# One weight load split over two DMA queues, and most filler matmuls left out, in a fused attention and soft-MoE kernel

## The chip, the cores and the metric

The kernel runs on one core of a Trainium2 chip. The core has five engines with instruction streams of their own: TensorE (PE in the profile, with its weight loads listed as PEld), VectorE (DVE), ScalarE (ACT), GpSimd (POOL) and SyncE (SP). They wait for each other through semaphores. Data comes from and goes to HBM through 16 DMA engines; a DMA is issued by SP, ACT or POOL, and the profile lists what each of these issued as a queue of its own: q1 for SP, q10 for ACT and q0 for POOL.

The metric is the device time of one execution, in microseconds; lower is better.

## The reference

The first stage is attention over 8 batches and 8 heads, 576 positions of 64 elements. Heads 0 to 3 look back over a window of 32 positions, heads 4 to 7 over every fourth of the last 128. The second stage is a soft mixture of experts on the 4608 tokens of 512 elements that come out: softmax weights over all tokens for 32 slots, two matmuls for each of 8 experts on its 4 slots, and softmax weights over the slots that spread the result back over the tokens.

```python
scores = scale * np.matmul(q, k.transpose(0, 1, 3, 2))
scores = np.where(masks[None, :, :, :], scores, -1000000000.0)
...
attn = attn / (np.sum(attn, axis=-1, keepdims=True) + 1e-09)
return np.matmul(attn, v).astype(np.float32)
...
logits = x @ phi
...
slot_input = d.T @ x
...
for e in range(E):
    h = np.maximum(slot_input[e] @ w1[e], 0.0)
    slot_out[e] = h @ w2[e]
...
return (c @ slot_out).astype(np.float32)
```

All inputs and the output are fp32 in HBM; on the chip the matmuls run in bf16.

## The kernel before

**Units.** Attention runs in 8 units: two batches times one kind of head (plain or dilated). `load_unit` (L433) brings q, k and v of a unit into one of three staging buffers `stg`, with three or six DMAs from POOL's queue that turn fp32 into bf16 on the way. The first unit is loaded in two halves of three DMAs each by `load_first` (L457). For each unit `st_T` (L627) transposes the staged data on TensorE (L643, L637) and ScalarE copies them to `TT` (L671); `st_S` makes scores (L689) and exponentials (L696); `st_V`, `st_P` and `st_X` make the output of attention; `st_L` makes the logits of a batch and adds to the slot inputs. A staging buffer can be loaded for unit u+3 when the transposes of unit u have read it, so the loads at L449 and L442 wait on POOL for TensorE.

**Weights.** All 16 expert weights stay in SBUF as bf16, each in a `home`: w1 of experts 0 to 6 in `WD`, the others in staging buffers and in `TT` once attention no longer needs them. `wload` (L479) and `wpair` (L860) load them from POOL's queue (L496, L874), in program order between the unit loads. The last of them, w2 of experts 6 and 7, come in pieces: first the columns 0 to 255, then the columns 256 to 511.

**The head.** One piece of a weight does not come through POOL. Half of w1 of expert 0 is loaded as fp32 by SP (L517, 1024 KB) into `pre`, which is the space of the later w1 of expert 6, and ScalarE turns it into bf16 in two activations (L533). `moe_phi` follows on SP's queue (L520, 64 KB).

**The tail.** When the slot inputs are complete (`psA`, then `siT`), the first expert matmul (L954) makes `h`, which is transposed to `hT` (L972). The second expert matmul is cut into groups by `ffn2` (L1015, matmuls at L1028), each of which waits for the weight pieces that it reads. `half(0)` (L1068) then scales the slot outputs of columns 0 to 255 (L1062), multiplies them with `expT` (L1080, L1093), scales by rows (L1063 on ScalarE, L1062 and L1105 on VectorE) and stores 1536 tokens' half rows from SP's and ScalarE's queues (L1057). `half(1)` does the same for columns 256 to 511 when the last weight piece has landed, and L1137 with its scalings makes the other 3072 tokens, stored in four large DMAs.

**The order.** Operations are not run in the order of the program text. `Prog.schedule` (L159) is a planner that runs when the kernel is built: it keeps a clock of its own for each engine, takes durations from the `cost` of each operation and lets DMAs run one after the other at 421.5 KB per microsecond, and places the operation that can start first; among those within `TOL` of each other the smaller `key` goes first. POOL and SP keep the order of the program. `emit` (L277) writes out the instruction streams with the semaphore waits.

**The fillers.** `FILL` (L28) is a list of stretches of the planner's clock. Whenever TensorE would be idle there for more than 0.4 us before its next operation, the planner puts matmuls of a constant tile `wrm` into the gap (L244 to L260). Their result is never read. Each entry gives start, end, the modes of the following operation for which it holds, the time to be left free in the gap, and the assumed duration of one matmul. On the chip nothing holds a filler back until its planned time: it follows the TensorE operation ahead of it.

```python
ts = max(free[e], lo)
if not (ts < hi and lo < t0 and o.mode in modes and t0 - ts > 0.4):
    continue
...
n = min(int((t0 - ts - slack) / each + 0.05), 64)
```

Of the kernel before, what the change touches and what calls it, by code (L numbers as in the profile page):

```python
# [24 lines left out]
NU = 8  # L25
QB = 96
HALO = 32
FILL = ((1.5, 9.0, "hf", 0.4, 0.43), (9.5, 13.5, "hf", 0.6, 0.25), (13.5, 116.0, "h", 0.3, 0.216),  # L28
        (13.5, 24.0, "rf", 0.3, 0.216), (116.0, 147.0, "hrfc", 0.15, 0.216))


class DmaSem:
# [85 lines left out]
class Prog:  # L118
# [6 lines left out]
    def op(self, e, fn, r=(), w=(), a=(), alloc=(), cost=0.5, key=0.0, mode="f",  # L125
           sem=None, nbytes=0, after=(), ndma=1, n=0, port=False):
        o = Op(e, fn, cost, key, mode)
        deps = list(after)
        for b in r:
            deps += b.ready  # L130
        for b in w:
            b.fresh()
            deps += b.prev
        for b in a:
            deps += b.prev
        seen = set()
        for d in deps:
            if d.id not in seen:
                seen.add(d.id)
                o.deps.append(d)  # L140
        for b in r:
            b.reads.append(o)
        for b in list(w) + list(a):
            b.ready.append(o)
        o.wr = [b for b in list(w) + list(a) if b.pool is not None]
        for b in list(r) + list(w) + list(a):
            if b.pool is not None and b not in o.touch:
                b.left += 1
                o.touch.append(b)
        o.alloc = list(alloc)  # L150
        o.sems = sem
        o.bytes = nbytes
        o.ndma = ndma
        o.n = 2 * n
        o.port = port
        self.ops.append(o)
        return o
# [171 lines left out]
def bass_dilated_sliding_attn__then__soft_moe_slots_kernel(  # L329
# [12 lines left out]
    op = P.op  # L342
# [159 lines left out]
    b_pre = Buf()  # L502
# [7 lines left out]
    for i in range(3):  # L510
# [3 lines left out]
    op("dve", lambda g: g.memset(wrm[:], 1.0), w=[b_wrm], cost=0.2, key=-1)  # L514
    load_first(0)
    pre = WD[:, 6, :].bitcast(F32)
    op("sp", lambda e: [e.dma_start(  # L517
        pre, moe_w1[0].rearrange("(p c) f -> p (c f)", c=4)[:, 0:2048])],
       w=[b_pre], cost=0.1, sem=DmaSem(nc, "s_pre"), nbytes=1048576)
    op("sp", lambda e: [e.dma_start(phi_st[:], moe_phi.rearrange("(c p) s -> p c s", p=128))],  # L520
       w=[b_phist], cost=0.1, sem=s_phi, nbytes=65536)
    op("dve", lambda g: g.memset(id0[:], 0.0), w=[b_id0], cost=0.3)
# [474 lines left out]
    for x in range(2):  # L997
        def rsum(t, x=x):
# [5 lines left out]
           cost=0.8, key=K1 + x, after=[ffn1] if x else [])  # L1004
    op("dve", lambda vv: vv.reciprocal(rtok[:], bank(rs)[:, 0:N_TOK // 128]), r=[rs], w=[b_rtok],
       cost=0.2, key=K1 + 1)
# [117 lines left out]
    for i, (n, hs) in enumerate(((4, (3,)), (4, (4,)), (8, (5, 6)), (8, (7, 8)))):  # L1124
# [7 lines left out]
        for j0 in range(0, n, 2):  # L1132
            po = tile(psum, 2)

            def pe(t, d0=d0, n=n, j0=j0, po=po):
# [3 lines left out]
            key = K1 + 60 + 10 * i + j0  # L1139
            op("pe", pe, r=b_so + b_expT, w=[po], alloc=[po], cost=0.45,  # L1140
               key=key)
# [24 lines left out]

    P.schedule(filler, FILL)

# [39 lines left out]
```

## Time and profile before

| | us |
|---|---|
| median of 3 runs | 176.25 |
| lowest, highest | 175.98, 176.44 |
| the profiled execution | 176.83 |
| its span, first to last instruction | 175.1 |

| engine | busy us | share of the span | instructions |
|---|---|---|---|
| PE | 142.7 | 81% | 2305 |
| PEld | 102.4 | 58% | 2305 |
| DVE | 108.8 | 62% | 259 |
| ACT | 96.5 | 55% | 147 |
| POOL | 65.2 | 37% | 111 |

The span is what the profile shows; the profiled execution took 1.73 us more than it. The DMAs moved 41.29 MB, counted where they were written: 30.41 MB in POOL's queue, 8.98 MB in SP's and 1.57 MB in ScalarE's. HBM was read for 61.93 MB and written for 9.44 MB, since what POOL's queue loads is fp32 in HBM and bf16 on the chip.

The fillers (L1155) are 79 matmuls of 128x512 elements with 22.9 us of TensorE's busy time, 436 ns each in the mean. Twenty of them start before 7.5 us, 13 between 12.4 and 18.3 us, three at 23.8 to 24.4 us, two at 118.0 and 119.5 us, and 41 from 123.2 to 146.4 us.

How to read it: busy shares are means over stages with different limits. The parts that matter here are the DMA engines' busy share along the span and the chain of waits that ended last.

### The profile page before, as it was taken

To read this page: it belongs to the slowest core of one execution; us is meant where nothing else is said; L and a number is where in the kernel's file an instruction comes from. 1 tells how busy PE (TensorE), PEld (TensorE's weight loads), DVE (VectorE), ACT (ScalarE), POOL (GpSimd) and SP (SyncE) were. 2 spreads that over 40 slices of the span, in tenths; PEclk is the share of its full clock that TensorE was granted. 3 is DMA by queue.
4 is the path that set the end of the run, shared out by engine and by line. 5 is a ranking of instruction groups with operands and counts; after the bars stand their busy time and mean duration, and the time that the engine had idled before them with its cause. 6 is when DMAs were issued, how large, how long until landed. Compare 5 with 4: busy or idle time off the path is not lost.

```text
span 175.1 us, 5257 instructions
## 1 busy us (share of the span) xinstructions
PE 142.7 (81%) x2305; PEld 102.4 (58%) x2305; DVE 108.8 (62%) x259; ACT 96.5 (55%) x147; POOL 65.2 (37%) x111
## 2 busy tenths in 40 slices
PE   7759886889896999996998899988999898599000
PEld 2245465677795887794986698765575344343000
DVE  6620494599789799969469979997403002379400
ACT  2332836697885778887378596853111002589300
POOL 7980649506963053951020839689000000000000
PEclk9997999999999999999699999999999999879955
DMA  5999998999999999999999999999999999999997
GB/s 176 249 215 213 221 231 187 221 212 213 233 212 203 219 208 219 233 206 207 218 212 212 217 215 217 213 215 217 215 204 210 201 195 196 295 331 404 449 419 299
DMA packets 12694, 41.29 MB, mean 236 GB/s; under 512 B 2208, under 2 KB 8864, under 8 KB 9120
## 3 DMA queue, kind: packets, MB, share of 16 engines
q0 software_dynamic: 8128, 30.41, 86.4%
q1 hardware_dynamic: 2912, 8.98, 13.3%
q10 hardware_dynamic: 1632, 1.57, 2.7%
q8 instruction: 18, 0.29, 0.6%
q14 instruction: 4, 0.03, 0.0%
HBM read 61.93 MB, written 9.44 MB: 408 GB/s over the span
## 4 chain that ended last, share of the span: by engine, by line
DMA 46%; PE 19%; DVE 10%; POOL 9%; ACT 7%; issue 1%; POOLq 0%; DVEq 0%
DMA stg<-in_v_dram 29%; DMA TT<-in_moe_w_dram 17%; ACT PT L696 5%; PE ps L643 4%; PE ps L637 4%; DVE WD L1062 3%; POOL TT L496 2%; PE ps L798 2%; PE ps L714 2%; PE ps L689 2%; POOL stg L449 2%; DVE XB L754 2%; PE ps L743 1%; PE ps L1093 1%; POOL mask_p L540 1%; POOL stg L442 1%
## 5 line engine op out<-in xcount | busy, mean ns | idle before, releaser
L696 ACT ACTIVATE PT<-ps 128x768 bf16<-128x768 f32 x48 | 36.8, 818 | 11.2 <-PE ps L689 10.9
L671 ACT ACTIVATE TT<-ps 128x864 f32<-128x864 f32 x32 | 28.1, 902 | 19.0 <-PE ps L643 11.7
L754 DVE TENSOR_TENSOR XB<-ps,RV 96x768 bf16<-96x768 f32 x32 | 30.2, 945 | 0.4
L1155 PE MATMUL ps<-wrm 128*128 128x512 bf16 x79 | 22.9, 436 | 1.1 <-DVE wrm L514 1.1
L719 DVE COPY VN<-ps 128x768 bf16<-128x768 bf16 x32 | 16.9, 538 | 10.4 <-PE ps L714 10.0
L643 PE MATMUL ps<-ident,stg 96*128 96x96 bf16 x288 | 15.4, 216 | 5.7 <-DMA stg<-in_v_dram 5.3
L1063 ACT ACTIVATE WD<-ps,rtok 128x256 f32<-128x256 f32 (+1 forms) x22 | 10.7, 555 | 16.1 <-PE ps L1080 14.8
L689 PE MATMUL ps<-TT 64*128 64x96 bf16 x384 | 15.9, 204 | 3.8 <-ACT PT L696 2.0
L643 PEld LDWEIGHTS ps<-ident,stg 96*128 96x128 bf16 x288 | 14.2, 104 | 7.3 <-DMA stg<-in_v_dram 6.3
L610 POOL COPY stg<-stg 96x576 f32<-96x576 f32 x24 | 16.8, 699 | 1.5
L743 PE MATMUL ps<-VN,PT 128*128 128x65 bf16 x384 | 16.7, 194 | 0.5 <-ACT PT L696 0.3
L714 PE MATMUL ps<-ident,TT 128*128 128x128 bf16 x192 | 16.3, 223 | 0.7 <-ACT TT L671 0.2
L743 PEld LDWEIGHTS ps<-VN,PT 128*128 128x128 bf16 x384 | 14.1, 98 | 2.2 <-DVE XB L754 0.8
L689 PEld LDWEIGHTS ps<-TT 64*128 64x128 bf16 x384 | 9.7, 94 | 9.7 <-ACT PT L696 3.9
L1155 PEld LDWEIGHTS ps<-wrm 128*128 128x128 bf16 x79 | 8.1, 111 | 11.7 <-issue 5.7
L704 DVE TENSOR_TENSOR PT<-PT,mask_d 128x768 bf16<-128x768 bf16 x24 | 12.9, 569 | 0.0
L714 PEld LDWEIGHTS ps<-ident,TT 128*128 128x128 bf16 x192 | 11.3, 100 | 2.7 <-DVE VN L719 0.5
L704 DVE TENSOR_TENSOR PT<-PT,mask_p 128x768 bf16<-128x768 bf16 x24 | 12.6, 541 | 0.2
L771 PE MATMUL ps<-ident,XB 96*128 96x96 bf16 x192 | 11.4, 206 | 1.4 <-DVE XB L754 1.2
L449 POOL DMA_DIRECT2D stg<-in_q_dram x8 | 4.1, 526 | 22.4 <-PE ps L643 22.4
L637 PE MATMUL ps<-ident,stg 96*128 96x96 bf16 x216 | 10.9, 206 | 1.5 <-POOL stg L610 1.2
L637 PEld LDWEIGHTS ps<-ident,stg 96*128 96x128 bf16 x216 | 9.8, 98 | 2.4 <-POOL stg L610 1.5
(99 smaller groups left out, 215.6 us busy)
## 6 DMA issues: line engine op xcount, KB each, us to landing
WD<-in_moe_w_dram POOLq DMA_DIRECT2D x6, 1024.0 KB, 27.0
stg<-in_moe_w_dram POOLq DMA_DIRECT2D x5, 1024.0 KB, 32.8
stg<-in_q_dram POOLq DMA_DIRECT2D x10, 288.0 KB, 18.1
stg<-in_k_dram POOLq DMA_DIRECT2D x10, 288.0 KB, 19.9
stg<-in_v_dram POOLq DMA_DIRECT2D x10, 288.0 KB, 21.9
out_dram<-WD SPq DMA_DIRECT2D x2, 1024.0 KB, 5.2
out_dram<-WD SPq DMA_DIRECT2D x1, 2048.0 KB, 8.4
out_dram<-stg SPq DMA_DIRECT2D x1, 2048.0 KB, 10.7
```

Of the source, the lines that this page charges most:

```text
L610: return g.tensor_copy(o_, i_)
L637: i_ = t.transpose(bankb2(pt, a)[:, 96 * kk:96 * kk + 96], il_ap(u, j, a)[:, 128 * kk:128 * kk + 128], ident[0:96, 0:96])
L643: i_ = t.transpose(bankb2(pt, a)[:, 96 * kk:96 * kk + 96], two[:, c, :], ident[0:96, 0:96])
L671: return ac.activation(d, sv, ACTF.Copy)
L689: i_ = t.matmul(pair(sc)[:, hx, QB * x:QB * x + QB], win(u, 1, h01, blk_, bpar)[64 * hx:64 * hx + 64], win(u, 0, h01, blk_, bpar)[64 * hx: ...
L696: op("act", lambda ac: ac.activation(sbt(pt)[:, 0:768].rearrange("p (x n) -> p x n", x=2), pair(sc)[:, :, 0:384], ACTF.Exp, scale=SCALE), ...
L704: return dv.tensor_tensor(p_, p_, m.unsqueeze(1).to_broadcast([128, 2, 384]), AluOp.mult)
L714: i_ = t.transpose(bankb(pv)[:, 128 * m:128 * m + 128], win(u, 2, h01, m, bpar), ident[:, :])
L719: op("dve", lambda dv: dv.tensor_copy(sbt(vn)[:, :, :, 0:64], bankb(pv)[:, 0:768].rearrange("p (m x d) -> p m x d", m=6, x=2)), r=[pv], w= ...
L743: i_ = t.matmul(pair(po)[:, bk, 65 * po_:65 * po_ + 65], sbt(pts[i])[:, o_:o_ + 128], sbt(vn)[:, m, half, 0:65], start=True, stop=True)
L754: op("dve", lambda dv: dv.tensor_tensor(sbt(xb)[:].rearrange("p m (x h d) -> p h x m d", x=2, h=2)[:, h01], pv()[:, :, :, 0:64], sbt(rv)[: ...
L1155: i_ = te.matmul(bank(t).rearrange("p (a x) -> p a x", a=4), wrm[:], wrm[:].unsqueeze(1).to_broadcast([128, 4, 128]), start=True, stop=True)
```

## The change

The fp32 half weight is loaded by two DMAs in place of one, partitions 0 to 63 by SP and 64 to 127 by ScalarE, each with a semaphore of its own. The two ScalarE activations at L533 wait for both. In the planner both have the key -2, ahead of all else, and ScalarE's DMA is taken to cost 0.6 us of ScalarE's time.

`FILL` has one entry in place of five. The fillers of the head, of attention and of the stretch up to 140.5 us of the planner's clock are left out, and so are those after 145.0. The new entry has the modes, the slack and the duration of the last old one. Since the planner no longer places the other fillers, the order of what it places afterwards can differ, too.

```diff
-FILL = ((1.5, 9.0, "hf", 0.4, 0.43), (9.5, 13.5, "hf", 0.6, 0.25), (13.5, 116.0, "h", 0.3, 0.216),
-        (13.5, 24.0, "rf", 0.3, 0.216), (116.0, 147.0, "hrfc", 0.15, 0.216))
+FILL = ((140.5, 145.0, "hrfc", 0.15, 0.216),)
...
     pre = WD[:, 6, :].bitcast(F32)
-    op("sp", lambda e: [e.dma_start(
-        pre, moe_w1[0].rearrange("(p c) f -> p (c f)", c=4)[:, 0:2048])],
-       w=[b_pre], cost=0.1, sem=DmaSem(nc, "s_pre"), nbytes=1048576)
+    for y, e_ in enumerate(("sp", "act")):
+        op(e_, lambda e, y=y: [e.dma_start(
+            pre[64 * y:64 * y + 64],
+            moe_w1[0].rearrange("(p c) f -> p (c f)", c=4)[64 * y:64 * y + 64, 0:2048])],
+           a=[b_pre], cost=0.1 if e_ == "sp" else 0.6, key=-2, sem=DmaSem(nc, f"s_pre{y}"),
+           nbytes=524288)
```

## The prediction

> **What bounds the kernel.** I read the row of DMA shares on the page first.
>
> ```profile
> PE   7759886889896999996998899988999898599000
> ...
> PEclk9997999999999999999699999999999999879955
> DMA  5999998999999999999999999999999999999997
> ```
>
> From the second slice on the DMA engines are busy for 90% or more of every slice but one and the last, while PE has gaps. The next view, the DMA queues in the window from 12 to 138 us, says whose work that is:
>
> ```profile
> q0 software_dynamic: 4046, 26.70, 102.0%
> ```
>
> POOL's queue, the loads, keeps 16 engines full (packets overlap a little, so 102%). The chain of waits agrees:
>
> ```profile
> 121.57 29.82 DMA TT<-in_moe_w_dram
> ...
> 151.44 0.32 PE ps L1028 x4
> ...
> 151.78 0.50 DVE so_sb L1062
> ```
>
> The last weight piece is issued at 121.57 and lands 29.8 us later, since 30 us of transfers are queued ahead of it. So the load stream ends at its first packet plus its own length, whatever PE does, as long as the queue never runs dry. After it 9.44 MB of stores go out; in the window from 155.50 to 174.30 the DMA share is 1.00 at 404 GB/s. The kernel is bound by DMA from about 2 us to the end. An edit can gain only where the engines are not moving bytes: the start, and a few notches at the hand-over from loads to stores.
>
> **Part 1, the split load.** The DMA queues in the windows 1.8 to 5.15 us and 5.15 to 8 us:
>
> ```profile
> q1 hardware_dynamic: 267, 1.04, 97.2%
> ```
>
> ```profile
> q0 software_dynamic: 82, 0.59, 102.1%
> q1 hardware_dynamic: 405, 0.07, 13.3%
> ```
>
> Until 5.15 us only SP's queue has packets; POOL's first load was issued at 1.38 us but its packets start at about 5.15. After that, SP's remainder (the end of the half weight, and phi) takes 13.3% of 2.85 us = 0.38 us of all engines away from the loads. The stretches of the first window show why it is late:
>
> ```profile
> 2.30:2.80 0.50, 0.50 (x2) 0.15 (x1) 0.31 (x8) 0.00 (x0) 0.50 (x2) 1.00 0.45 147
> 3.80:4.30 0.50, 0.50 (x3) 0.17 (x2) 0.50 (x1) 0.00 (x0) 0.50 (x2) 1.00 0.96 410
> ```
>
> (The last two columns are DMA share and GB/s.) The transfer runs at 147 GB/s at first and at 410 later. 1.04 MB at 410 are 2.54 us; it took 3.35, so the start costs 0.8 us. If a second queue fills that start, all of SP's work is done before 5.15 and the loads end 0.38 us earlier; it can't be more, since POOL's first packet is set by POOL. At the other end, if the second queue pays a slow start of its own for its half, 0.4 us is added. ScalarE's issue should take about what its stores at L1057 take (0.55 us) and may come behind its table load (0.81 to 2.09 us), but the queue has 3 us to become useful. I take -0.25: two thirds of the gain, since the engines' low rate in this start shows room.
>
> [...]
>
> What moves with it: phi stands behind half as much on SP's queue; ScalarE's two conversions (1.05 us each, now from 7.02) come up to 1 us earlier; ScalarE's next work is at 11.84, so nobody waits. The table load (1.28 us) may slip by 0.55 us, still ahead of the conversions. With the cover gone (conversions late by over 2.7 us) the first evacuation at L671 would be late. POOL's order is untouched.
>
> **Part 2, the head without fillers.** The timeline of PE in the head:
>
> ```profile
> 10.87 1.84 PE L643 MATMUL ps<-ident,stg 96*128 96x96 bf16 x36 [3.13 <-DMA stg<-in_v_dram]
> 12.51 3.69 PE L1155 MATMUL ps<-wrm 128*128 128x512 bf16 x9
> 16.03 1.70 PE L643 MATMUL ps<-ident,stg 96*128 96x96 bf16 x36
> ```
>
> Despite the fillers the clock fell at 12.29 us (granted 0.50 up to 15.71), and nine of them stretched to 3.69 us. The second half of the first unit, issued last at 4.66 with at most 10.3 us to landing, was there by 15.0; PE began at 16.03. Without fillers PE starts cold: 36 such transposes took 2.50 us at 85.45, half of it or more at clock 0.50, so about 10.87 + 2.5 = 13.4 and 15.0 + 2.5 = 17.5, against 17.73 now. No loss. If the clock stays at half for another 3.4 us, PE loses 1.7 us. This is covered: PE meets the DMA stream again at 32.34 and 83.5 us (in the chain it waits for in_v_dram there), and POOL's loads from L496 and L874 land 17.9 us or more after issue, so a buffer released 2 us late still leaves the queue full. Cost 0; without that cover, up to 1.7 us.
>
> **Part 3, attention and the expert stage.** Five fillers between 20 and 120 us don't matter. From 123 to 136.5 us there are 15, beside work that ends with hT at 134.4. The second expert matmul then waits for weights (136.53), and what must be done by 146.7 is only 1.9 + 2.2 us of L1028. So the planner's changed order, or a clock dip, has some 7 us of cover before the first store is late. Cost 0.
>
> **Part 4, the last fillers.** Now 19 run from 138.38 to 142.58. If the planner's clock is near the trace's, those of the new entry start at 140.5 in the plan, so (4.2 - 2.1 - 0.15)/0.216 = 9 remain; on the chip they follow at once (138.4 to 140.3), then PE idles for 2 us. What a half-idle stretch does is in the stretches of 3.41 us around two dips (PE's busy time is the second number, the granted clock the third from the end):
>
> ```profile
> 80.56:83.97 3.41, 1.83 (x44) 1.50 (x41) 3.36 (x8) 2.05 (x3) 0.00 (x0) 1.00 0.92 193
> 83.97:87.39 3.42, 3.42 (x45) 3.42 (x43) 1.02 (x2) 1.35 (x2) 0.00 (x0) 0.50 1.03 215
> 148.83:152.24 3.41, 1.61 (x17) 0.70 (x14) 1.39 (x3) 1.99 (x5) 0.00 (x0) 1.00 1.06 277
> 152.24:155.65 3.41, 3.33 (x14) 2.11 (x15) 1.90 (x4) 2.59 (x6) 0.00 (x0) 0.50 0.97 328
> ```
>
> 3.41 us with 1.83 or 1.61 us of PE work were each followed by 3.41 us at half clock. In the gap left, 3.41 us would hold as little as 1.5 us, so a dip somewhere in 142 to 147.5 is likelier than not. The group of L1028 from 142.58 to 144.8 (2.2 us) then takes 3 to 4.4 us; it has to be done before the last pieces of half 0 at 146.72, so 0 to 0.3 us of lateness comes through. The first store packets, at 149.3, overlap the end of the loads (DMA share 1.24 from 149 to 150), which hides some 0.5 us. Bounds 0 and +1.1 (below); I take +0.1.
>
> [...]
>
> **Sum.** -0.25 + 0 + 0 + 0.1 = -0.15. The profiled execution has a span of 175.1 and took 176.83, 0.58 above the median; with the same 1.73 around it I expect a span of 174.95 and 176.68 for an execution like it, and for the median 176.25 - 0.15 = **176.1 us**.
>
> **Rivals.**
> *No gain at the start* (15%): two queues share what one had, or ScalarE's DMA comes behind its table load. For it: the engines look busy, 97.2%, in the slow start. Against: 147 GB/s there. 176.25 + 0.1 = 176.35. [...]
>
> *The hand-over closes up* (27%). Stretches of DMA share now:
>
> ```profile
> 150.25:150.50 0.25, 0.09 (x4) 0.00 (x0) 0.00 (x0) 0.25 (x2) 0.00 (x0) 1.00 0.62 172
> 151.25:151.50 0.25, 0.07 (x4) 0.07 (x4) 0.00 (x0) 0.19 (x1) 0.00 (x0) 1.00 0.54 176
> 155.25:155.50 0.25, 0.25 (x2) 0.15 (x1) 0.12 (x1) 0.25 (x2) 0.00 (x0) 0.50 0.31 103
> ```
>
> That is 0.25 x (0.38 + 0.46 + 0.69) = 0.38 us unused. From 150.5 to 151.1 POOL's queue holds 8.4% of the engines, about one of 16: one straggler, and one 16 KB instruction fetch (q8, 6.0% of 1 us = 0.96 us of one engine) fell at 149.4. Some 68 fillers fewer are 136 PE instructions fewer; 4610 of them go with 18 fetches, about 256 each, so this fetch moves by half a period. If the straggler and the notches go and the head gives its 0.38: 176.25 - 0.76 = 175.5. Against: the fetch can hit another engine's tail as well.
>
> *Half 0 comes late on a cold clock* (18%), the slower side. If the dip lasts from 142.3 to 149: L1028 4.4 in place of 2.2 us, ending 146.7; two fillers 0.85; the two last groups 0.3 each, 148.2 in place of 147.0; L1080 and L1093 2.75 (as they took at 152.32 on the cold clock) in place of 1.48. First stores 1.4 us late, less 0.5 hidden, and the later ones a little more: +1.1, with the head's -0.25: 177.1. It decides once stores start after about 149.9. Against: a dip lasts 3.41 us in every case seen, and PE is busy in it.
>
> **Chances.** Forecast 40%, rivals 15, 27 and 18. A measurement of this kernel tells about 0.3% (0.53 us) from no change. The forecast and the first rival lie inside; so faster 0.30 (27, and 3 from the forecast's edge), same 0.50, slower 0.20 (18, and 2 from that edge). The range runs from a little beyond the fast rival to the slow one, 175.3 to 177.1, since cases of both signs hold 45%; the forecast alone has 175.8 to 176.5.
>
> **What would show it.** Head: SP's and ScalarE's packets gone by 5.2 us and in_v_dram's first landing up to 0.4 us before 10.8; wrong if they end at 5.7 or later. PE: transposes at half clock at 10.9, the unit done near 17.5. Loads: last landing near 151.1. Tail: granted clock 0.50 around 142 to 147, first store packets before 149.9, DMA share near 1.0 after. A DMA share under 0.9 in any slice before 148 us would prove the cover wrong; a last landing earlier by over 0.6 us, or a shorter store stream, the forecast.

## The result, and the profile after

| | before | after |
|---|---|---|
| median of 20 runs, us | 176.57 | 178.24 |
| lowest, us | 175.91 | 177.63 |
| the profiled execution, us | 176.83 | 177.94 |
| its span, us | 175.1 | 176.2 |
| mean granted TensorE clock | 0.944 | 0.948 |

The changed kernel is slower: the ratio of its time to the time before is 1.0089, 95% interval 1.0070 to 1.0109. The medians are of all runs, while ratios, here and below, leave out the runs that fell into a slower state. I had expected -0.15 us; the medians differ by +1.67 us and the profiled executions by +1.11.

The rows of the page of the changed kernel (40 slices of 4.4 us):

```profile
PE   0017737899989899899898979988769988599000
...
PEclk9999999999999999999999999999997899969755
DMA  5999999999999999998999999999999999999996
```

The DMA engines are as busy as before, though PE's head is now empty. So the kernel is still bound by DMA from about 2 us to the end, and the time must have come in through what the engines moved or how fast. The chain of waits says where it appears:

```profile
127.30 25.55 DMA TT<-in_moe_w_dram
...
152.89 0.32 PE ps L1030 x4
```

(Start, duration.) The last weight piece lands at 152.85, where it landed at 151.39: 1.46 us later. It is issued 5.7 us later than before (127.30 against 121.57) but the queue is still 25 us long, so the issue is not what makes it late. From the landing to the end of the span it takes 23.35 us, where it took 23.71. In these two profiled executions the whole loss is in the load stream, and the tail gave back a third of a microsecond.

The stream itself did not get longer. POOL's queue has 85.9% of 176.2 us = 151.4 us of packets; before it had 86.4% of 175.1 = 151.3. It begins later: its first packet starts at 6.58 us, not at 5.15. That is +1.43. The head, from the timeline of the changed kernel:

```profile
0.81 0.60 ACTq L517 DMA_DIRECT2D WD<-in_moe_w_dram  x1
0.82 0.60 SPq L517 DMA_DIRECT2D WD<-in_moe_w_dram  x1
...
12.61 3.06 PE L645 MATMUL ps<-ident,stg 96*128 96x96 bf16 x36 [12.61 <-DMA stg<-in_v_dram]
...
24.15 0.20 DVE L576 CAST phi_pad<-phi_st 128x64 bf16<-128x64 f32 x1 [16.52 <-DMA phi_st<-in_moe_phi_dram]
```

Both halves are issued at once. The first attention data lets PE start at 12.61, where it was 10.87. The last line is a wait that was not there before, and it looks like the culprit: `phi` lands 22.6 us after its issue in place of 6.5, and VectorE stands for 16.5 us behind it. What the two halves do to the engines is in the DMA queues of the window from 0 to 6.5 us, and in two of the stretches that were shown of before:

```profile
q10 hardware_dynamic: 80, 0.52, 33.7%
q1 hardware_dynamic: 60, 0.49, 33.3%
```

```profile
2.30:2.80 0.50, 0.00 (x0) 0.00 (x0) 0.31 (x8) 0.00 (x0) 0.50 (x2) 1.00 0.56 98
3.80:4.30 0.50, 0.00 (x0) 0.00 (x0) 0.50 (x1) 0.00 (x0) 0.50 (x2) 1.00 1.00 213
```

(The last two columns are DMA share and GB/s.) At 3.8 us the engines are fully busy, 1.00, but move 213 GB/s where they moved 410. ScalarE's 64 packets of 8 KB take 33.7% of 6.5 us x 16 engines = 35.0 us, or 0.55 us each; the median one of before took 0.31, the mean of all with the slow start 0.40. The two queues use 67.0% of 6.5 us = 4.36 us of all engines before POOL gets one; SP alone used 97.2% of 3.35 = 3.26 us. That is 1.10 us more, and the first packet starts 0.39 us later (2.21 against 1.82): together 1.49 us, against 1.43 seen at POOL's first packet and 1.46 at the last landing. The last of SP's slow packets ends at 7.38 us; 5.7 or later was the prediction's sign that this part had failed.

Two theories stood after this. **Slow halves:** a transfer to 64 neighbouring partitions runs at half the rate, whatever queue carries it, and POOL's stream stands behind it. **The late table:** the halves are harmless, and what costs is `phi`, which now lands at 24 us and delays attention. A third one was that two queues hinder each other.

### The profile page after: what moved, and what is told of

Its sections match the earlier page's. It is cut to its first block, busy times and chain, and to the rows that moved or that the text cites. A ratio compares the mean times of both kernels' runs of the same rounds, so it can differ in the third digit from the quotient of the medians.

```text
span 176.2 us, 5119 instructions
## 1 busy us (share of the span) xinstructions
PE 130.1 (74%) x2234; PEld 101.2 (57%) x2235; DVE 111.0 (63%) x259; ACT 96.6 (55%) x147; POOL 66.6 (38%) x111
## 3 DMA queue, kind: packets, MB, share of 16 engines
q0 software_dynamic: 8128, 30.41, 85.9%
## 4 chain that ended last, share of the span: by engine, by line
PE 33%; DMA 27%; DVE 18%; ACT 8%; POOL 4%; issue 3%; POOLq 0%; DVEq 0%; SPq 0%
DMA TT<-in_moe_w_dram 14%; DMA phi_st<-in_moe_phi_dram 13%; PE ps L639 8%; ACT PT L698 5%; PE ps L645 5%; DVE XB L756 4%; DVE PT L706 4%; PE ps L745 4%; PE ps L716 4%; PE ps L691 3%; PE ps L800 3%; DVE WD L1064 3%; PE ps L773 3%; POOL TT L495 2%; ACT TT L673 2%
## 5 line engine op out<-in xcount | busy, mean ns | idle before, releaser
L645 PE MATMUL ps<-ident,stg 96*128 96x96 bf16 x288 | 16.8, 225 | 14.7 <-DMA stg<-in_v_dram 13.7
L645 PEld LDWEIGHTS ps<-ident,stg 96*128 96x128 bf16 x288 | 15.4, 109 | 15.4 <-DMA stg<-in_v_dram 13.9
L716 PE MATMUL ps<-ident,TT 128*128 128x128 bf16 x192 | 17.3, 231 | 3.9 <-DVE VN L721 3.3
L745 PE MATMUL ps<-VN,PT 128*128 128x65 bf16 x384 | 17.8, 198 | 2.3 <-DVE PT L706 0.9
L612 POOL COPY stg<-stg 96x576 f32<-96x576 f32 x24 | 17.7, 735 | 1.5
L745 PEld LDWEIGHTS ps<-VN,PT 128*128 128x128 bf16 x384 | 15.0, 101 | 3.9 <-issue 2.4
L716 PEld LDWEIGHTS ps<-ident,TT 128*128 128x128 bf16 x192 | 12.0, 103 | 6.2 <-DVE VN L721 4.2
L706 DVE TENSOR_TENSOR PT<-PT,mask_d 128x768 bf16<-128x768 bf16 x24 | 14.9, 652 | 0.0
L448 POOL DMA_DIRECT2D stg<-in_q_dram x8 | 4.2, 527 | 22.8 <-PE ps L645 22.8
L639 PE MATMUL ps<-ident,stg 96*128 96x96 bf16 x216 | 12.2, 220 | 0.3 <-issue 0.3
L773 PEld LDWEIGHTS ps<-ident,XB 96*128 96x128 bf16 x192 | 9.6, 100 | 4.1 <-DVE XB L756 2.9
L639 PEld LDWEIGHTS ps<-ident,stg 96*128 96x128 bf16 x216 | 11.4, 106 | 0.8 <-issue 0.5
L786 ACT ACTIVATE XT<-ps 128x576 bf16<-128x576 bf16 x16 | 10.0, 651 | 1.7 <-PE ps L773 1.4
```

The lines of the kernel that those rows point to most:

```text
L612: return g.tensor_copy(o_, i_)
L639: i_ = t.transpose(bankb2(pt, a)[:, 96 * kk:96 * kk + 96], il_ap(u, j, a)[:, 128 * kk:128 * kk + 128], ident[0:96, 0:96])
L645: i_ = t.transpose(bankb2(pt, a)[:, 96 * kk:96 * kk + 96], two[:, c, :], ident[0:96, 0:96])
L706: return dv.tensor_tensor(p_, p_, m.unsqueeze(1).to_broadcast([128, 2, 384]), AluOp.mult)
L716: i_ = t.transpose(bankb(pv)[:, 128 * m:128 * m + 128], win(u, 2, h01, m, bpar), ident[:, :])
L745: i_ = t.matmul(pair(po)[:, bk, 65 * po_:65 * po_ + 65], sbt(pts[i])[:, o_:o_ + 128], sbt(vn)[:, m, half, 0:65], start=True, stop=True)
```

## The experiments

Ratios are to the kernel before, run on the same chip, with 95% intervals.

**e1, the split alone, and e2, the fillers alone.** e1 is the changed kernel with the five old entries of `FILL`:

```diff
-FILL = ((140.5, 145.0, "hrfc", 0.15, 0.216),)
+FILL = ((1.5, 9.0, "hf", 0.4, 0.43), (9.5, 13.5, "hf", 0.6, 0.25), (13.5, 116.0, "h", 0.3, 0.216),
+        (13.5, 24.0, "rf", 0.3, 0.216), (116.0, 147.0, "hrfc", 0.15, 0.216))
```

> The split load of the change with all five FILL entries of before. If the split is the cause: the load stream starts about 1.4 us late (POOL's first packets near 6.6 in place of 5.15 us), the last weight piece lands near 152.8, and the time is within 0.3 us of the changed kernel, 1.4 to 1.7 us over before. If the missing fillers are the cause: within 0.3 us of before. If each has a share, in between.

e2 is the kernel before with the reverse of this edit.

> The single-entry FILL of the change with the one DMA of before. If the split is the whole cause: within 0.3 us of before, POOL's first packets at 5.15 and the last landing near 151.4. If the missing fillers cost something (a cold clock in the head or near 142 us): up to 1.1 us over before. If leaving them out frees time: up to 0.4 us under before.

e1 took 1.0144 (1.0100 to 1.0187), e2 0.9979 (0.9954 to 1.0005). The split is the whole loss; leaving out fillers costs nothing and may gain 0.2%. In e1 POOL's first packet starts at 6.47 us, in e2 at 5.15. The loss of e1 is some 2.5 us, where 1.4 to 1.7 were expected; its interval just overlaps that of the changed kernel, and what the rest is stays open.

**e3, e4: which property of the split.** e3 gives SP the even partitions and ScalarE the odd ones:

```diff
-            pre[64 * y:64 * y + 64],
-            moe_w1[0].rearrange("(p c) f -> p (c f)", c=4)[64 * y:64 * y + 64, 0:2048])],
+            pre[y:128:2],
+            moe_w1[0].rearrange("(p c) f -> p (c f)", c=4)[y:128:2, 0:2048])],
```

> The changed kernel, but SP loads the even partitions and ScalarE the odd ones. Partition theory (64 neighbouring partitions take in 8 KB packets at half the rate): the slow stretch goes, GB/s near 410 in the window in which the changed kernel has about 240, the half weight is complete near 5.2 us, and 1.2 to 1.6 us of the loss come back. Queue theory (two queues disturb each other whatever they write): GB/s stays near 240, the half weight is complete at 7 us or later, and the time is within 0.3 us of the changed kernel.

e4 leaves the halves as they are and issues both from SP:

```diff
-    for y, e_ in enumerate(("sp", "act")):
+    for y, e_ in enumerate(("sp", "sp")):
```

> The changed kernel, but both halves (partitions 0 to 63, then 64 to 127) go by SP's queue. Partition theory: still about 240 GB/s while the half weight is loaded, complete at 6.5 us or later, time within 0.4 us of the changed kernel. Queue theory: near 410 GB/s, complete near 5.5 us, 1.2 to 1.6 us faster than the changed kernel.

e3: 0.9975 (0.9950 to 1.0000). e4: 1.0169 (1.0116 to 1.0222). One view tells them apart, the stretch from 3.5 to 5.0 us. Before, then the changed kernel:

```profile
3.50:5.00 1.50, 1.50 (x5) 0.51 (x4) 1.50 (x3) 0.00 (x0) 1.50 (x4) 1.00 0.96 392
```

```profile
3.50:5.00 1.50, 0.00 (x0) 0.00 (x0) 1.50 (x3) 0.00 (x0) 1.50 (x4) 1.00 0.90 202
```

and e3, then e4:

```profile
3.50:5.00 1.50, 0.00 (x0) 0.00 (x0) 1.50 (x3) 0.00 (x0) 1.50 (x4) 1.00 0.97 399
```

```profile
3.50:5.00 1.50, 0.00 (x0) 0.00 (x0) 1.50 (x3) 0.00 (x0) 1.50 (x4) 1.00 1.15 242
```

At like shares the engines move 392 and 399 GB/s where the partitions of each DMA lie across the whole range, and 202 and 242 where they are 0 to 63 and 64 to 127. (In e4 POOL's packets are among these from 3.88 us on; SP alone, from 2.20 to 3.80 us, moves 261 GB/s, and its 8 KB packets take 0.55 us in the mean.) Two queues didn't hinder each other here (e3 has two, 399 GB/s), and one queue didn't help (e4 has one, 242).

e4 also showed where the cover ends. There `phi` landed 27.2 us after its issue, the first L1030 matmul started at 144.1 us (changed kernel: 141.9, before: 136.5), and the stores were not ready when the loads ran out, as its stretches show:

```profile
151.00:152.00 1.00, 1.00 (x10) 0.90 (x11) 0.63 (x2) 0.74 (x3) 0.00 (x0) 1.00 0.20 26
152.00:152.50 0.50, 0.50 (x6) 0.27 (x5) 0.50 (x2) 0.50 (x3) 0.00 (x0) 1.00 0.09 12
```

(DMA share 0.20 and 0.09.) So e4 pays twice, and is not a clean measure of the halves alone.

e4 shows one more thing. Its load stream is late at the end (the last packet ends at 152.82 us, in e2 at 150.21) although POOL's first packet came early, at 3.88. So the early first packet did not bring the end forward; I put that down to the engine time that the slow packets take, 0.55 us each.

**e5, other borders.** SP takes partitions 32 to 95, ScalarE 0 to 31 and 96 to 127 in two DMAs:

```diff
-    for y, e_ in enumerate(("sp", "act")):
+    for y, (e_, lo, hi) in enumerate((("sp", 32, 96), ("act", 0, 32), ("act", 96, 128))):
...
-            pre[64 * y:64 * y + 64],
+            pre[lo:hi],
```

> The changed kernel, but SP loads partitions 32 to 95 and ScalarE 0 to 31 and 96 to 127 in two DMAs. If the slow packets come from which side of partition 64 a DMA writes (one side alone is slow): SP's 64 packets of 8 KB, 32 on each side, take about 0.31 to 0.40 us each, ScalarE's, one side at a time, about 0.55. If any 64 neighbouring partitions are slow: SP's take about 0.55. If it is two queues in flight: all about 0.55.

0.9990 (0.9957 to 1.0024): the loss is gone, POOL's first packet starts at 5.56 us. As a test of single packets it was inconclusive, since both queues were in flight together and both show a mean of some 0.48 us. It does bear on a rival that nothing else separates, that a half is slow because it reads a narrower stretch of HBM: SP's DMA here reads 64 neighbouring rows too, and its packets take 0.48 us where the changed kernel's halves took 0.54 and 0.58. That speaks against the rival but doesn't settle it.

**e6, one DMA, on ScalarE, and e7, none at all.** In e6 the half weight is one DMA again, issued by ScalarE (first two lines, against the kernel before). In e7 w1 of expert 0 comes whole through POOL as bf16 (last two lines), and the fp32 half and its two conversions are not there; both have the short `FILL`:

```diff
-    op("sp", lambda e: [e.dma_start(
+    op("act", lambda e: [e.dma_start(
...
-                wload(n_, ((4, 8, 0, 512),) if n_ == "w10" else ((0, 8, 0, 512),))
+                wload(n_, ((0, 8, 0, 512),))
```

> The changed kernel's FILL, and the half weight in one DMA of 128 partitions by ScalarE's queue, phi alone on SP's. If the partitions are the cause, ScalarE's queue does what SP's did: near 410 GB/s, half weight complete near 5.7 us, last landing 150.5 to 151.5, time within 0.4 us of the kernel with the single-entry FILL alone. If ScalarE's queue itself is slower: more than 0.6 us over that.

> The changed kernel's FILL, no fp32 half weight at all: w1 of expert 0 comes whole by POOL's queue. Where POOL's first packets start then tells what sets their time. If POOL sets it (as the prediction had it): 5.15 us, with the engines idle until then, and the load stream ends 2.5 us later. If they stand behind SP's packets on the engines: 3 to 4 us, and the stream ends 0.5 to 1.3 us later than with the single-entry FILL alone.

e6: 0.9976 (0.9951 to 1.0001). e7: 0.9969 (0.9942 to 0.9996). Neither the queue nor the issuing engine made a difference here (e2 has 0.9979), nor, within these intervals, the route of this half weight. (e7's loads end 1.26 us after e2's, 151.47 against 150.21, inside the 0.5 to 1.3 expected; its profiled execution was the slowest of its ten, 177.23 us against a median of 176.60.) e7 shows one more thing, in the DMA queues from 2 to 5 us:

```profile
q0 software_dynamic: 46, 0.36, 82.6%
```

POOL's packets run from 2.73 us there. In the kernel before they ran from 5.15: not because POOL was slow to start (it issues its first load at 1.38 us in both), but because SP's megabyte was on the engines ahead of them.

**e8, phi first.** The changed kernel with SP's two DMAs in the other order:

```diff
     load_first(0)
+    op("sp", lambda e: [e.dma_start(phi_st[:], moe_phi.rearrange("(c p) s -> p c s", p=128))],
+       w=[b_phist], cost=0.1, sem=s_phi, nbytes=65536)
```

(and the same two lines taken out behind the halves.)

> The changed kernel with phi issued on SP ahead of its half of the weight. If phi's late landing (24 us) has a share in the time: phi lands by 6 us, VectorE is not held up, hT is ready near 135 in place of 141, and the time falls by over 0.5 us. If the time is set by the load stream alone: hT comes early all the same, but the last weight piece lands 0 to 0.4 us earlier and the time is within 0.4 us of the changed kernel.

1.0067 (1.0034 to 1.0100). The theory of the late table falls as the main cause: the DMA issues of e8 (KB, us from issue to landing) show `phi` early and the kernel still slower than before. A share of up to 0.2% (1.0089 against 1.0067) can't be told from noise.

```profile
WD<-in_moe_w_dram SPq DMA_DIRECT2D x1, 512.0 KB, 10.4
...
phi_st<-in_moe_phi_dram SPq DMA_DIRECT2D x1, 64.0 KB, 3.4
```

Now SP's half is what lands last of the two, and the load stream's last packet ends at 153.01 us, in the changed kernel at 152.57; it was expected up to 0.4 us earlier, not later. POOL's first packet came at 3.99 here. So the slow packets cost about as much in either place (1.0067 and 1.0089).

**e9, quarters.** Four DMAs of 32 partitions, all from SP:

```diff
-    for y, e_ in enumerate(("sp", "act")):
-        op(e_, lambda e, y=y: [e.dma_start(
-            pre[64 * y:64 * y + 64],
+    for y in range(4):
+        op("sp", lambda e, y=y: [e.dma_start(
+            pre[32 * y:32 * y + 32],
...
```

> The changed kernel with the half weight in four DMAs of 32 partitions, all by SP. If a DMA is slow because it writes on one side of partition 64 alone, 32 partitions are as slow as 64: 8 KB packets of about 0.55 us, time within 0.6 us of the kernel with both halves of 64 on SP. If the rate goes with the number of partitions: packets of about 1.1 us and 2 us or more over it.

1.0209 (1.0117 to 1.0300; two runs). Its stretches:

```profile
3.50:5.00 1.50, 0.00 (x0) 0.00 (x0) 1.50 (x3) 0.00 (x0) 1.50 (x4) 1.00 1.03 193
...
153.00:154.00 1.00, 1.00 (x11) 0.90 (x10) 0.77 (x2) 0.88 (x3) 0.00 (x0) 1.00 0.00 0
```

Thirty-two partitions are as slow here as 64 (193 GB/s against 202, 0.52 us a packet in the mean), not slower again by half. (POOL's packets are among these from 3.97 us on.) The rest of its loss is e4's second price, larger: no DMA at all from 152 to 154 us, since the second expert matmul began only at 146.0.

**e10, the split by columns.** Two queues and two DMAs, each over all 128 partitions and half of the columns:

```diff
-            pre[64 * y:64 * y + 64],
-            moe_w1[0].rearrange("(p c) f -> p (c f)", c=4)[64 * y:64 * y + 64, 0:2048])],
+            pre[:, 1024 * y:1024 * y + 1024],
+            moe_w1[0].rearrange("(p c) f -> p (c f)", c=4)[:, 1024 * y:1024 * y + 1024])],
```

> The changed kernel, but each of the two DMAs loads all 128 partitions and half of the columns (4 KB packets). Partition theory: no loss from two queues, half weight complete by 6 us, last landing 150 to 151.5, time 1.2 to 1.8 us under the changed kernel. If splitting over two queues costs something of its own: in between.

0.9965 (0.9944 to 0.9985), median 176.06 us, and once more 0.9964 (0.9935 to 0.9993) as e15 below. It is faster than both kernels. Its stretch:

```profile
3.50:5.00 1.50, 0.00 (x0) 0.00 (x0) 1.50 (x3) 0.00 (x0) 1.50 (x4) 1.00 0.99 385
```

The rate is back, with packets of half the size. The time is 1.2% under that of the changed kernel, 2.2 us, somewhat more than the 1.2 to 1.8 expected. POOL's first packet starts at 5.11 us, 0.04 before the old one: splitting itself is worth nearly nothing. The gain is that of e2, e3 and e6, which have the same short `FILL`.

**e11, e12: the fillers, in parts.** Both are the kernel before with another `FILL`. e11 keeps only the old last entry, e12 the first four and the new last one:

```diff
+FILL = ((116.0, 147.0, "hrfc", 0.15, 0.216),)
```

```diff
-        (13.5, 24.0, "rf", 0.3, 0.216), (116.0, 147.0, "hrfc", 0.15, 0.216))
+        (13.5, 24.0, "rf", 0.3, 0.216), (140.5, 145.0, "hrfc", 0.15, 0.216))
```

> One DMA by SP as before; of FILL only the last entry of before (116 to 147 us), so the head and attention run without fillers. If the missing head fillers matter for the time: slower or faster than before by over 0.4 us. If the head is covered by the load stream: within 0.4 us of before.

> One DMA by SP as before; the entries of before up to 116 us, and the change's short entry (140.5 to 145) in place of 116 to 147. If what the single-entry FILL gains (0.2% by its run) comes from the tail's fillers being fewer: 0.3 to 0.5 us under before, last landing near 150.5. If a cold clock there costs: slower than before. If neither: within 0.3 us.

e11: 1.0049 (1.0012 to 1.0085). e12: 1.0067 (1.0024 to 1.0109). Here 36 and 34 fillers fewer make it slower, wherever they are left out, but 70 fewer (e2) make it, if anything, faster. That has no order as long as fillers are taken for what they are meant to be. It has one by the time of the last fetch of 16 KB of instructions through a DMA engine (queue q8): 141.7 us in e2, 149.4 before, 156.1 in e12, 159.2 in e11. I take these fetches for PE's, since their number goes with PE's instructions (matmuls and weight loads together): 17 for 4470 of them (e2), 18 for 4538 and more (e11, e12, before).

**e13, e14, e15: the number alone.** e15 is e10 unchanged; e13 and e14 put 36 and 14 fillers ahead of PE's first transpose, where PE waits for data anyway:

```diff
-FILL = ((140.5, 145.0, "hrfc", 0.15, 0.216),)
+FILL = ((1.5, 9.0, "hf", 0.4, 0.24), (140.5, 145.0, "hrfc", 0.15, 0.216))
```

(0.6 in place of 0.24 in e14.)

> The split by columns of e10_split_columns, with 36 fillers put ahead of TensorE's first transpose and nothing else changed; TensorE is idle there, so no later work has to wait for them. Theory (the number of TensorE instructions decides when its last piece of instruction code is fetched, and a fetch between 155 and 160 us takes one DMA engine away from the stores): 2271 matmuls as in e12_head_fill_kept, so a last fetch of instructions at 155 to 160 us, and 0.3 to 0.8% above e10_split_columns, about 1.000 to 1.004 of the kernel before. Rival (fillers matter only through the clock or the order around them): last fetch wherever it falls, ratio 0.9965 like e10_split_columns, within 0.2%.

> The same with 14 fillers ahead of TensorE's first transpose, 2249 matmuls. Theory of the fetch: 22 matmuls fewer than in e13_36_at_the_start move the fetch from about 157 to some 5 to 8 us later, inside the store stream still or past TensorE's last work; 0 to 0.6% above e10_split_columns. Rival: like e10_split_columns, within 0.2%.

> e10_split_columns once more, unchanged, beside the other two on the same chip. Both theories: 0.9965 of the kernel before, within 0.2%, last fetch of instructions at about 140.5 us.

e13: 1.0052 (1.0026 to 1.0078), 177.69 us. e14: 1.0008 (0.9972 to 1.0044), 177.24 us. e15: 0.9964 (0.9935 to 0.9993), 175.96 us. The intervals of e13 and e15 don't touch: 36 matmuls that delay nobody cost 0.9%, some 1.6 us, a little more than the 0.8% at most that was expected. e14 is less sure, since its interval overlaps that of e15: five of its 12 runs took 175.9 to 176.5 us, like nearly all of e15's, and seven 177.0 to 178.4. Both e13 and e14 have an 18th fetch, which e15 has not. Apart from the fillers all engines run the same operations in the same order as in e10, so a changed order is not the cause. In e13 PE's head even runs better (its timeline):

```profile
1.13 10.17 PE L1157 MATMUL ps<-wrm 128*128 128x512 bf16 x36 [1.13 <-DVE wrm L513]
11.14 1.70 PE L645 MATMUL ps<-ident,stg 96*128 96x96 bf16 x36
14.51 1.85 PE L645 MATMUL ps<-ident,stg 96*128 96x96 bf16 x36 [1.67 <-DMA stg<-in_v_dram]
```

Its transposes take 1.70 and 1.85 us per 36, in e10 3.06 each; the row of the granted clock has 9 in the first three slices of both, so that row doesn't show why. e13 is done with the first unit at 16.36 us, where e10 is done at 17.87, and the load stream ends alike (150.40 and 150.45 in e13 and e15). The difference is at the very end. The DMA queues of e13 from 155 to 166 us hold one instruction fetch, at 161.5 (164.1 in e14), in the middle of the stores:

```profile
q8 instruction: 1, 0.02, 0.5%
```

That is 0.5% of 11 us x 16 = 0.9 us of one engine. From 155.5 to 172.5 us the two kernels differ little: the DMA share is 1.02 in e13 and 1.03 in e10, at 415 and 417 GB/s, so the lower granted clock of e13 (0.895 against 0.920 in the mean) doesn't hold up the stores. Its last stretches, with those of e10 below them, do differ:

```profile
172.50:173.00 0.50, 0.00 (x0) 0.00 (x0) 0.00 (x0) 0.00 (x0) 0.00 (x0) 0.50 0.92 393
173.00:173.50 0.50, 0.00 (x0) 0.00 (x0) 0.00 (x0) 0.00 (x0) 0.00 (x0) 0.50 0.09 33
173.50:174.00 0.50, 0.00 (x0) 0.00 (x0) 0.00 (x0) 0.00 (x0) 0.00 (x0) 0.50 0.08 33
174.00:174.50 0.50, 0.00 (x0) 0.00 (x0) 0.00 (x0) 0.00 (x0) 0.00 (x0) 0.50 0.08 33
```

```profile
172.50:173.00 0.50, 0.00 (x0) 0.00 (x0) 0.00 (x0) 0.00 (x0) 0.00 (x0) 0.50 1.23 524
173.00:173.50 0.50, 0.00 (x0) 0.00 (x0) 0.00 (x0) 0.00 (x0) 0.00 (x0) 0.50 0.02 0
```

For 1.5 us 33 GB/s are moved, a sixteenth of 524: by this, an estimate, one engine finishes alone, and the kernel waits for it. That this is the engine that fetched is an inference, since no view names the engine. e11, with its fetch at 159.2, has the same three stretches of 33 GB/s from 173.5 on, and e14 has three from 173.0 to 175.0. e12 has one, at 175.5. The length of the store phase separates all four from the rest: from the end of POOL's last packet to the end of the last store packet e11 to e14 take 24.1 to 24.6 us, and all other kernels 22.8 to 23.4, but for e4 and e9 with their gaps. e12 is late by more than that, since its loads ended at 152.42 us, 1.3 after those of before; why is not shown, and a lower granted clock (0.907 in the mean, 0.944 before) is not excluded there.

## Why the prediction was wrong, step by step

**Part 1, the split load, is the step that failed.** It was put at -0.25 us, bounds -0.38 and +0.4, "since the engines' low rate in this start shows room". It measured about +1.4: POOL's first packet +1.43, the last landing +1.46. Two premises under the term were wrong. The first was silent: that a DMA over 64 neighbouring partitions moves bytes at the rate of one over 128 (the stretch from 3.5 to 5.0 us has 202 GB/s against 392). No row of before shows one, so the rate should have been bounded too; the bound +0.4 held only a second slow start. (POOL's loads of q, k and v do go to 32 neighbouring partitions, but they could not show it: 9216 B in 0.70 us a packet, and 8192 B in 0.63 us for its weight loads over 128, are both some 210 GB/s over 16 engines, about what the halves have.) Doubling the 2.54 us that the megabyte takes at 410 GB/s would have given a bound of +2.5. The second was spoken: "it can't be more, since POOL's first packet is set by POOL". e7 has POOL's packets at 2.73 us; what set 5.15 was SP's transfer, so what is added ahead of it comes through (1.49 us by the packets, 1.43 seen). The gain was misread as well: the 0.38 us behind 5.15 are not the end of the half weight but nearly all `phi` (0.07 MB in 405 packets, and `phi` is 64 KB), which the split leaves as it is.

The runs show which splits are slow: 202 in place of 392 GB/s for partitions 0 to 63 beside 64 to 127, 193 for blocks of 32, against 399 for every second partition and 385 for all partitions with half of the columns each; with 32 to 95 beside the rest the loss was gone as well (e5, 0.9990). What makes the blocks slow is not shown. A second issuing engine gained nothing by itself: in e10 POOL starts 0.04 us earlier (5.11 against 5.15). For the split as it was made, the partitions decided and not the issuing engines.

The slow start that I meant to fill (147 GB/s at 2.3 us) is not a matter of one queue: with two queues the same stretch has 98 in the changed kernel and in e10 POOL's first packet is no earlier.

**What moves with it.** **phi** "behind half as much on SP's queue" was wrong in its consequence. It landed 22.6 us after its issue, since its 512 packets of 128 B came to stand beside POOL's packets (0.55 MB in 76 packets from 6.5 to 9 us, 7 KB and 0.57 us each in the mean). From 11 to 24 us SP's queue had 411 packets and POOL's 452, so about one of the small ones went with one of the large. If each of 32 small packets on an engine (512 over 16, if they are spread evenly) waits for one large one, 0.57 us apiece make an estimate of 18 us; the trace has 16.9 us from phi's first packet at 7.26 to its landing. The start of the kernel before looks different: POOL's packets took no turns with the packets that SP had queued but came from 5.15 us on, as those ran out (the last one of 8 KB ends at 5.71), and why they came in between in e4, from 3.88 on, is not shown. VectorE's wait of 16.5 us behind `phi` is real, but e8 shows that it doesn't set the time. ScalarE's conversions came later, not earlier: the table load went from 0.81 to 8.36 us, behind the landing of the half weight, and they ran from 9.65 to 11.65 us in place of 7.02 to 9.02. ScalarE's next work was at 14.26, so this cost nothing.

**Part 2, the head without fillers**, cost 0, as forecast. The first transposes took 3.06 us per 36, not 2.50, and in e2 the first unit was done at 18.1 us, not at 17.5; nobody waited. That they are slow because PE "starts cold" is not shown: the row of the granted clock has 9 there, in every slice of the changed kernel up to 132 us.

**Part 3, the cover of some 7 us**, held. In the changed kernel the second expert matmul begins 5.4 us later (141.9 against 136.5) and the loads still set the end; e4 at 144.1 and e9 at 146.0 are beyond the cover. The sign that I named for a broken cover, a DMA share under 0.9 before 148 us, came in one slice (79.3 to 83.7 us, just under 0.90), as it had before (26.3 to 30.6 us, 0.89), so it proves nothing; and in the head the share was no sign of health either: the engines were full, at half the rate. (The trace has 16 fillers from 123 to 136.5 us, not 15; nothing hangs on it.)

**Part 4, the last fillers**, was put at +0.1 for a clock dip. The changed kernel has no dip there, as the stretch shows:

```profile
142.00:147.50 5.50, 5.50 (x65) 2.38 (x57) 0.00 (x0) 0.00 (x0) 0.00 (x0) 1.00 1.44 196
```

PE was late and so busy throughout. In the profiled executions of e2 and e10, where it was not late, PE was busy for 4.05 and 3.38 of these 5.50 us and the granted clock stayed 1.00 too. But e15, which is e10 unchanged, has the dip, and in the shape that was inferred (stretches of 3.41 us as in the prediction):

```profile
138.01:141.42 3.41, 0.98 (x5) 0.25 (x3) 0.00 (x0) 0.00 (x0) 0.00 (x0) 1.00 1.16 192
141.42:144.83 3.41, 3.38 (x24) 1.60 (x24) 0.00 (x0) 0.00 (x0) 0.00 (x0) 0.50 1.45 196
```

So the dip comes in some executions of a kernel and not in others. Where it came it shows no price: the loads ended at 150.45 us in e15 and at 150.67 in e10, and the ratios are 0.9964 and 0.9965. The nine fillers that the prediction left over are there in the changed kernel, e2 and e10.

**The rivals.** "No gain at the start" was nearer than the forecast, with the wrong mechanism. "Half 0 comes late on a cold clock", the only slower one, gave the right side for a wrong reason; its premise that a dip lasts 3.41 us doesn't hold in later traces either (e10 is at 0.50 from 126.04 to 132.87 us). "The hand-over closes up" was right in e2 and e10 (a last landing 0.9 and 0.4 us earlier than before), but paid 0.4 and 0.6 us of its 0.76, and in the changed kernel it is the third of a microsecond that the tail gave back. Its instruction fetch, which it let move "by half a period", was the better idea: with 70 fillers fewer the 18th fetch is gone.

## What to carry to other kernels

When a DMA that should run at some 400 GB/s is split over queues, split it by columns or by every second partition (385 and 399 here), not at partition 64 or into blocks of 32 neighbours, which ran at 202 and 193 here. A busy DMA share says nothing of bytes (0.90 went with 202 GB/s here and 0.96 with 392), so read GB/s beside it. If a queue's first packet is late, look at what is on the engines ahead of it before calling it the queue's own start (POOL's came at 5.15 us behind SP's megabyte, at 2.73 without it). A change of the number of instructions can move the time of the instruction fetches: 36 matmuls more moved the last one from 139.0 to 161.5 us here, in among the stores, and with it came a loss of 0.9% with nothing else changed (e13 against e15); check where the last fetch falls before crediting or blaming the edit.

## What was not expected of the hardware

**Blocks of partitions.** A packet of 8 KB took 0.55 us in place of 0.31 when the DMA's partitions were 0 to 63 or 64 to 127. With both in flight on two queues, which together write all 128 partitions, the rate was still 202 GB/s; why is not shown.

**Two issues at the same moment.** ScalarE's packets began at 2.21 us and SP's at 3.73, though both DMAs were issued at 0.8. Before, SP's began at 1.82.

**The instruction fetch.** Over the kernels without slow halves (e5 is in between), a late last fetch goes with a long time; among the early ones, and among the late ones, the order is not strict:

| kernel | last fetch on q8, us | ratio to before |
|---|---|---|
| e15, e10 | 139.0, 140.5 | 0.9964, 0.9965 |
| e3, e2, e6 | 140.9, 141.7, 141.7 | 0.9975, 0.9979, 0.9976 |
| e7, e5 | 144.3, 144.7 | 0.9969, 0.9990 |
| before | 149.4 | 1 |
| e12, e11 | 156.1, 159.2 | 1.0067, 1.0049 |
| e13, e14 | 161.5, 164.1 | 1.0052, 1.0008 |

Up to 145 us, while the loads run, a last fetch cost nothing that these runs can tell (ratios of 0.9964 to 0.9990). Among the stores the kernel with it is some 1.6 us longer (e13 against e15), more than the 0.9 us for which it holds its engine; where the rest comes from stays open. Whether the fetch of before, at 149.4 and close to the end of its loads, is why e2 is 0.2% faster is not tested. Fetch times are those of one profiled execution of each kernel.
